# Scores and their gradients in groups of four chunks, bf16 scores out of PSUM, and the rescale of P on GpSimd, in the backward pass of a two-branch layer

## The chip, the core and the metric

The kernel runs on one core of a Trainium2 chip. The metric is device time in microseconds (us) of one execution. The engines are named as in the profile: PE is TensorE (its weight loads are PEld), DVE is VectorE, ACT is ScalarE, POOL is GpSimd, SP is the queue that issues most DMAs.

## The reference

One layer with two branches, forward and all gradients, for x of shape 2 × 4000 × 144 in bf16 (B = 2, T = 4000, D = 144, K = 5). The attention branch is what the change is about:

```python
xa = _layernorm(x, axis=-1)
qkv = jnp.einsum('btd,de->bte', xa, w_qkv)
q, k, v = (qkv[..., :D].copy(), qkv[..., D:2 * D].copy(), qkv[..., 2 * D:].copy())
scores = jnp.einsum('btd,bsd->bts', q, k) * D ** (-0.5)
p = _softmax(scores, axis=-1)
attn = jnp.einsum('bts,bsd->btd', p, v)
glob = jnp.einsum('btd,de->bte', attn, w_att_out)
```

The local branch (GELU, a layer norm, a 5-tap convolution over time, a product) gives `loc`; both are joined, pass another 5-tap convolution, and a last matmul adds them to x. The kernel returns that output and, from `grad_out`, the gradients of x and of the seven weights.

## The kernel before, in words

**Tiles.** The two batches are done one after the other, with the merge of the first overlapping the start of the second. In a batch T is cut into NB = 32 row-tiles of PB = 125 tokens. The scores of a tile, 125 × 4000, are made in eight chunks of CH = 500 columns, worked on as four pairs c2 = 0 to 3. A pair lies in one PSUM buffer `ps` of two banks, one bank a chunk; there are two such buffers (`ps_sg`), three smaller ones for all else (`ps_w`: X, projections, transposes, local steps) and one for Y and Z (`ps_yz`).

**The contraction over D = 144** has 16 rows more than the array's 128. The first 128 are `xaT_m` (columns of all tokens) against `qt` slot 0 or 2; the other 16 lie at partitions 96 to 111 of the array `R`, whose other rows hold zeros or are met by zeros: the narrow rows of a tile are put at columns 96 to 111 of a zeroed buffer `qrr`, transposed into slots 1 and 3 of `qt`, and multiplied as a second full 128-row matmul (L741, L791).

**The loop** (`phase_att`) goes over t = 0 to 32, in eight steps each. The first four make the scores of tile t (`S_pair`): four matmuls, then DVE writes −S into `Pbuf` with a running row minimum (L745 for the first pair, L747 for the others), and ACT makes the exponential from PSUM into `Pbuf` with the minimum so far as bias (L748), so the score buffer is held until ACT is done. The last four make dP = dY·V' of tile t − 1 (`dP_pair`): four matmuls, then one DVE pass (dP − delta) · P into `Sbuf` (L794). Steps 2 and 3 also hold the two halves of Y(t − 1) = P·[x, 1] (L768), after which DVE makes 1/rowsum and delta (L774, L778), ACT makes `yn` and the scaled queries `QBs` (L780, L782). At step 3, `rescale(t)` brings the first three pairs of P to the last minimum: factors f by ACT (L753), two pairs on DVE (L757), one on ACT (L759), and then one DMA transpose of the tile's P into `PT` (L760), which Y reads. Steps 6 and 7 hold the halves of Z(t − 2) from `ST` (L810), the DMA transpose of `Sbuf`.

**Between them** stand the X groups (L849): for three blocks of tokens, products of P and S of two tiles with `QBs`, twelve matmuls or more, added by DVE to the accumulator `acc` in SBUF (L855); the projection of the next tile's queries (`jit_mm`, L707 to L711, and its transposes `jit_tr`, L722); and the local branch, whose steps (`local_units`, 16 groups of two tiles a batch) are spread over the tiles by a running count.

**The order.** The code's order is the priority order; a scheduler takes from it, for each engine, the next instruction that is ready by its estimates. The engines' queues run in order. `high_priority` and `issue_after`, which the change uses, move instructions in that order.

## Time and profile before

| what | us |
|---|---|
| three runs | 1459.54, 1456.56, 1458.52 (median 1458.52) |
| the profiled execution, its own time | 1457.65 |
| its span from first to last instruction | 1455.9 |
| granted clock of TensorE, mean | 0.99 of full speed |

The page of the profile gives for each engine the busy time and its share of the span, and the span in 40 slices, each digit the busy tenths of a slice. A group row reads: line, engine, operation, output<-inputs, shapes, count | busy us, mean ns of one | idle time of the engine just before them and what ended it. A row of a source line gives ns as minimum/median/maximum, then the first and last start in us. A timeline row gives start us, duration us, engine, line and operation; behind it in brackets idle time and its releaser. A matmul's duration includes its way through the array, so what a matmul costs in a stream is read from start to start. A waits row reads: who waited for whom, us in total, times, longest.

### The profile page before, as it was taken

The page shows a single profiled execution, that of the slowest core. Times are in us where ns is not written, and L with a number is a line of the kernel's source. Part 1 is how long each engine was busy: PE and PEld are TensorE (multiplying, and loading weights), DVE is VectorE, ACT ScalarE, POOL GpSimd, SP SyncE. Part 2 cuts the span into 40 slices and gives each one's busy share as a digit, 9 for nine tenths or more (in the row PEclk, how much of TensorE's full clock was granted, in tenths as well). Part 3 has the DMA queues.
Part 4 walks back from the last instruction along what each step waited for, and adds up shares of the span by engine and source line. Part 5 has one row for each costly group of instructions (what it writes and reads, how often), then busy time and mean ns, then how long its engine had stood idle before and what let it go on. Part 6 is the DMA issues. An engine that isn't in the chain of part 4 may idle for free. (4 is left out here: it accounts for less than half of the span.)

```text
span 1455.9 us, 38963 instructions
## 1 busy us (share of the span) xinstructions
PE 1371.7 (94%) x16186; PEld 1180.2 (81%) x16186; DVE 1179.7 (81%) x2747; ACT 863.0 (59%) x1636; POOL 289.0 (20%) x515
## 2 busy tenths in 40 slices
PE   5999999999999999988887999999999999999898
PEld 3778888888888888887865888888888888888797
DVE  7799988888898988869457988888888888887754
ACT  6766666666666665525456666666666666554281
POOL 8411011111111110148212012111111111111420
PEclk9999999999999999999999999999999999999999
DMA  3586767666666666774236676666676666776712
GB/s 109 104 139 118 119 119 122 123 123 112 110 119 114 117 109 123 125 170 131 81 67 121 123 123 116 110 122 126 113 122 117 122 110 119 132 123 115 209 37 64
DMA packets 559391, 170.37 MB, mean 117 GB/s; under 512 B 542447, under 2 KB 554113, under 8 KB 559172
## 3 DMA queue, kind: packets, MB, share of 16 engines
q1 hardware_dynamic: 553578, 155.57, 58.0%
q0 software_dynamic: 5088, 12.11, 3.3%
q8 instruction: 126, 2.06, 0.6%
q14 instruction: 51, 0.42, 0.1%
q10 hardware_dynamic: 548, 0.21, 0.1%
HBM read 21.04 MB, written 14.12 MB: 24 GB/s over the span
## 5 line engine op out<-in xcount | busy, mean ns | idle before, releaser
L794 DVE SCALAR_TENSOR_TENSOR Sbuf<-ps,delta,Pbuf 125x1000 bf16<-125x1000 f32 x256 | 320.2, 1256 | 31.1 <-PE ps L791 29.0
L849 PE MATMUL X<-QBs,Sbuf 125*125 125x144 bf16 x2048 | 303.0, 226 | 6.5 <-DVE acc L855 2.7
L849 PE MATMUL X<-QBs,Pbuf 125*125 125x144 bf16 x2048 | 301.9, 226 | 0.0
L849 PEld LDWEIGHTS <-Pbuf 125*125 125x125 bf16 x2048 | 262.0, 137 | 15.2 <-issue 10.8
L849 PEld LDWEIGHTS <-Sbuf 125*125 125x125 bf16 x2048 | 261.9, 137 | 5.1
L855 DVE TENSOR_TENSOR acc<-X,acc 125x432 f32<-125x432 f32 x372 | 204.3, 552 | 36.5 <-PE X L849 35.7
L740 PE MATMUL ps<-xaT_m,qt 128*125 128x500 bf16 x512 | 193.2, 377 | 9.9 <-ACT Pbuf L748 6.7
L790 PE MATMUL ps<-xaT_m,qt 128*125 128x500 bf16 x512 | 191.8, 375 | 9.1 <-ACT Pbuf L748 6.1
L741 PE MATMUL ps<-R,qt 128*125 128x500 bf16 x512 | 192.3, 376 | 0.6 <-DVE R L357 0.4
L791 PE MATMUL ps<-R,qt 128*125 128x500 bf16 x512 | 191.0, 373 | 0.0
L768 PEld LDWEIGHTS <-PT 125*125 125x125 bf16 x2048 | 149.2, 138 | 28.2 <-DMA PT<-Pbuf 10.1
L768 PE MATMUL yz<-xa_aug,PT 125*125 125x145 bf16 x2048 | 152.4, 228 | 8.6 <-DMA PT<-Pbuf 8.5
L810 PEld LDWEIGHTS <-ST 125*125 125x125 bf16 x1984 | 143.8, 138 | 16.8
L810 PE MATMUL yz<-xa_aug,ST 125*125 125x144 bf16 x1984 | 147.7, 228 | 0.0
L745 DVE TENSOR_SCALAR_CACHE_REDUCE Pbuf<-ps 125x1000 bf16<-125x1000 f32 x64 | 76.7, 1198 | 23.7 <-PE ps L741 23.1
L595 POOL TENSOR_TENSOR A_dwc<-l_fl,A_dwc 128x512 f32<-128x512 f32 (+2 forms) x48 | 35.7, 743 | 295.9 <-ACT l_fl L594 295.9
L741 PEld LDWEIGHTS <-qt 128*125 128x125 bf16 x512 | 70.4, 137 | 28.7 <-issue 9.2
L791 PEld LDWEIGHTS <-qt 128*125 128x125 bf16 x512 | 69.6, 136 | 29.6 <-issue 9.3
L740 PEld LDWEIGHTS <-qt 128*125 128x125 bf16 x512 | 70.2, 137 | 22.2 <-issue 1.8
L790 PEld LDWEIGHTS <-qt 128*125 128x125 bf16 x512 | 69.7, 136 | 22.7 <-DVE Sbuf L794 2.1
L465 POOL TENSOR_SCALAR l_a<-l_sq 125x576 bf16<-125x576 bf16 x32 | 21.5, 671 | 299.5 <-ACT l_sq L463 260.2
L814 ACT ACTIVATE zn<-yz,rl 125x144 bf16<-125x144 f32 x64 | 24.1, 376 | 95.0 <-PE yz L810 94.9
(801 smaller groups left out, 3089.8 us busy)
## 6 DMA issues: line engine op xcount, KB each, us to landing
Yn_d<-yn SPq DMA_DIRECT2D x64, 35.2 KB
Zn_d<-zn SPq DMA_DIRECT2D x64, 35.2 KB
ug_d<-ugr SPq DMA_DIRECT2D x32, 70.3 KB
xo<-in_x_dram SPq DMA_DIRECT2D x16, 140.6 KB
out_dram<-dxo SPq DMA_DIRECT2D x16, 140.6 KB
go_h<-in_grad_out_dram POOLq DMA_DIRECT2D x4, 504.0 KB, 6.7
Zn<-Zn_d SPq DMA_DIRECT2D x4, 504.0 KB
PT<-Pbuf SPq DMA_TRANSPOSE x64
```

The costliest lines, as they stand in the source:

```text
L595: nc.gpsimd.tensor_tensor(acc, fl[0:rows, 0:n], acc, op=ALU.add)
L740: nc.tensor.matmul(ps[:, h, 0:CH], qt[:, 0, :], xaTm[:, cs], start=True, stop=False)
L741: nc.tensor.matmul(ps[:, h, 0:CH], qt[:, 1, :], R[:, cs], start=False, stop=True)
L745: nc.vector.tensor_scalar(pdst, src, -1.0, None, op0=ALU.mult, op1=ALU.min, accum_out=nm[:, 0:1])
L768: nc.tensor.matmul(Y, PT[0:PB, j, 0:PB], xaa[:, j, 0:D + 1], start=(j == 0), stop=(j == NB - 1))
L790: nc.tensor.matmul(ps[:, h, 0:CH], qt[:, 2, :], xaTm[:, cs], start=True, stop=False)
L791: nc.tensor.matmul(ps[:, h, 0:CH], qt[:, 3, :], R[:, cs], start=False, stop=True)
L794: nc.vector.scalar_tensor_tensor(sdst, ps[:, :, 0:CH].rearrange("p h (a b) -> p h a b", b=PB), DL[i][:], psrc, op0=ALU.subtract, op1=ALU.mult)
L810: nc.tensor.matmul(Z, ST[0:PB, j, 0:PB], xaa[:, j, 0:D], start=(j == 0), stop=(j == NB - 1))
L814: nc.scalar.activation(zn[:, 0:D], Z, ACT.Copy, scale=RL.pop(i)[:])
L849: nc.tensor.matmul(X[:, jj, :], l, r, start=(n_ == 0), stop=(n_ == len(ops) - 1))
L855: nc.vector.tensor_tensor(av, X[:, 0:nj, :], av, op=ALU.add)
```

## The change

- **Groups of four** (`quad`): a pair of S of tile t and a pair of dP of tile t − 1 are made together. First the four 128-row matmuls (L744), then the four remainder matmuls (L750), each of only 16 rows. The narrow rows of the tokens are copied by eight more SP transfers a batch into a new array `XR`, chunk c at partitions 32·(c mod 4); the tile's narrow rows are put at the four matching places by two POOL copies (`rems`), so that the four matmuls lie in four different groups of 32 partitions and in four banks. The pairs of dP run in the order 1, 0, 3, 2.
- **Scores leave PSUM after DVE** (`S_exp`): DVE writes −S as bf16 with the pair's own minimum (L770, a constant in place of the earlier minimum), a small DVE operation takes the running minimum (L772), and ACT makes the exponential in place in SBUF (L773).
- **dP** (`PdP`): for three pairs ACT copies dP from PSUM into `Sbuf` as bf16 (L780) and DVE multiplies by P in SBUF, 1024 wide with the padding (L782); for the fourth DVE multiplies straight from PSUM (L778). delta is no longer subtracted there; it enters as −delta/rowsum (`nd`, L815) into Z (`ty` on ACT, then L846 on DVE in place of ACT) and into `QBs`, which takes four POOL operations now (L822 to L826).
- **Rescale** on POOL, three operations of 1024 (L791), except for a batch's last tile and the first two of the second batch.
- **Order**: Y of t − 1 stands at the end of a tile after the last group, Z of t − 2 after the second group, the `ST` transpose goes in two halves; the end of a batch is reordered so that its last dP doesn't wait for Y.
- **Local steps**: six of ACT's element-wise operations a group of two tiles go to POOL (two of 576, four of 144 elements).

The core of the diff:

```diff
+            for c in (2 * g, 2 * g + 1):
+                nc.sync.dma_start(S.XR[32 * (c % 4):32 * (c % 4) + DR, (c // 4) * CH:(c // 4 + 1) * CH], S.R[96:112, c * CH:(c + 1) * CH])
...
-        nc.scalar.activation(q_[:], th[:], ACT.Copy, scale=0.5, bias=0.5)
+        nc.gpsimd.tensor_scalar(q_[:], th[:], 0.5, 0.5, op0=ALU.mult, op1=ALU.add)
...
+        def quad(work, stacked=True):
+            pp = [ps_sg.tile([PB, 2, 512], F32, tag="sg", name="ps") for _ in range(len(work) // 2)]
+            for r, (i, h, c) in enumerate(work):
+                mm = nc.tensor.matmul(pp[r // 2][:, r % 2, 0:CH], QT[i][:, 3 * h, :], xaTm[:, c * CH:(c + 1) * CH], start=True, stop=False)
+            with tc.issue_after(mm.ins), tc.high_priority():
+                for r, (i, h, c) in enumerate(work):
+                    q = c % 4 if stacked else 3
+                    rs = slice(32 * q, 32 * q + DR)
+                    xr = XR[rs, (c // 4) * CH:(c // 4 + 1) * CH] if stacked else R[rs, c * CH:(c + 1) * CH]
+                    nc.tensor.matmul(pp[r // 2][:, r % 2, 0:CH], QT[i][rs, 1 + (q // 2 + h) % 2, :], xr, start=False, stop=True)
...
-                nc.vector.tensor_scalar(pdst, src, -1.0, nm[:, c2 - 1:c2], op0=ALU.mult, op1=ALU.min, accum_out=nm[:, c2:c2 + 1])
-            nc.scalar.activation(pdst, src, ACT.Exp, bias=nm[:, c2:c2 + 1], scale=1.0)
+            nc.vector.tensor_scalar(pdst, src, -1.0, 3.0e38, op0=ALU.mult, op1=ALU.min, accum_out=nm[:, o:o + 1])
+            if c2:
+                nc.vector.tensor_tensor(nm[:, c2:c2 + 1], nm[:, c2 - 1:c2], nm[:, o:o + 1], op=ALU.min)
+            nc.scalar.activation(pdst, pdst, ACT.Exp, bias=nm[:, c2:c2 + 1], scale=-1.0)
...
-            nc.vector.scalar_tensor_tensor(sdst, ps[:, :, 0:CH].rearrange("p h (a b) -> p h a b", b=PB), DL[i][:], psrc, op0=ALU.subtract, op1=ALU.mult)
+            if direct:
+                nc.vector.tensor_tensor(pv(Sbuf, i % NDB, c2), src, pv(Pbuf, i % NPB, c2), op=ALU.mult)
+            else:
+                nc.scalar.copy(pv(Sbuf, i % NDB, c2), src)
+                sc = Sbuf[0:PB, i % NDB, c2 * 1024:(c2 + 1) * 1024]
+                nc.vector.tensor_tensor(sc, sc, pchunk(i % NPB, c2), op=ALU.mult)
...
+                if not quick:
+                    nc.gpsimd.tensor_scalar(p_, p_, f[:, c2:c2 + 1], 1.0, op0=ALU.mult, op1=ALU.mult)
...
+            products(0)
+            if ok(t - 3):
+                zt_tr(t - 3)
+            loc(0.25)
+            if ok(t + 1):
+                jit_mm(t + 1)
+            loc(0.5)
+            x(1)
+            products(1)
+            for h in range(2):
+                if ok(t - 2):
+                    Z_half(t - 2, h)
+            st_half(0)
+            x(1)
+            loc(0.6)
+            if t < NB:
+                products(2)
+            if ok(t + 1):
+                jit_tr(t + 1)
+            x(1)
+            loc(0.95)
+            x(1)
+            if t < NB:
+                products(3)
+                for h in range(2):
                     if ok(t - 1):
+                        Y_half(t - 1, h)
+            loc(1.0)
             x(6)
+            st_half(1)
+            if t < NB:
+                rescale(t, t == NB - 1)
```

**How it moves instructions.** TensorE before, at the start of a tile: the end of an X group, one pair of S (`xaT_m` the 128 rows, `R` the remainder, `ps_7145` the score buffer), with the transposes of zn (L822) behind it.

```order
L849 MATMUL X_7116<-QBs_120,Pbuf_116 125x144
L740 LDWEIGHTS qt_6998
L740 MATMUL ps_7145<-xaT_m_64,qt_6998 125x500
L741 LDWEIGHTS qt_6998
L741 MATMUL ps_7145<-R_65,qt_6998 125x500
L740 LDWEIGHTS qt_6998
L740 MATMUL ps_7145<-xaT_m_64,qt_6998 125x500
L741 LDWEIGHTS qt_6998
L741 MATMUL ps_7145<-R_65,qt_6998 125x500
L822 LDWEIGHTS zn1_128
```

Each chunk's remainder follows its 128-row matmul directly. TensorE after, at the same place, from the third matmul of the group on: `ps_7520` and `qt_7362` are the scores of tile t, `ps_7521` and `qt_7041` the dP of tile t − 1, `XR` the copied narrow rows.

```order
L744 LDWEIGHTS qt_7041
L744 MATMUL ps_7521<-xaT_m_64,qt_7041 125x500
L744 LDWEIGHTS qt_7041
L744 MATMUL ps_7521<-xaT_m_64,qt_7041 125x500
L750 LDWEIGHTS qt_7362
L750 MATMUL ps_7520<-XR_66,qt_7362 125x500
L750 LDWEIGHTS qt_7362
L750 MATMUL ps_7520<-XR_66,qt_7362 125x500
L750 LDWEIGHTS qt_7041
L750 MATMUL ps_7521<-XR_66,qt_7041 125x500
L750 LDWEIGHTS qt_7041
L750 MATMUL ps_7521<-XR_66,qt_7041 125x500
```

The four remainder matmuls now stand in one row, with nothing between them, and two score buffers are taken in one go. DVE before, from the end of Y (rl, dj) through the dP passes of a tile to the next tile's first scores:

```order
L774 RECIPROCAL rl<-yz 125x1
L778 SCALAR_TENSOR_TENSOR dj,delta<-yz,rl,qb_122 125x144
L794 SCALAR_TENSOR_TENSOR Sbuf<-ps,delta,Pbuf 125x8x125
L757 TENSOR_SCALAR Pbuf<-Pbuf,f 125x8x125 x2
L855 TENSOR_TENSOR acc<-X,acc 125x3x144
L794 SCALAR_TENSOR_TENSOR Sbuf<-ps,delta,Pbuf 125x8x125 x2
L855 TENSOR_TENSOR acc<-X,acc 125x3x144
L855 TENSOR_TENSOR acc<-X,acc 125x144
L794 SCALAR_TENSOR_TENSOR Sbuf<-ps,delta,Pbuf 125x8x125
L855 TENSOR_TENSOR acc<-X,acc 125x3x144
L745 TENSOR_SCALAR Pbuf,nm__8734<-ps 125x8x125
```

DVE after, from a tile's last group (its scores L770, its direct dP product L778) through the end of Y to the next tile's first groups:

```order
L770 TENSOR_SCALAR Pbuf,nm__7530<-ps 125x8x125
L778 TENSOR_TENSOR Sbuf<-ps,Pbuf 125x8x125
L772 TENSOR_TENSOR nm__7530<-nm__7530 125x1
L810 RECIPROCAL rl<-yz 125x1
L813 SCALAR_TENSOR_TENSOR dj,delta<-yz,rl,qb_122 125x144
L815 SCALAR_TENSOR_TENSOR nd<-delta,rl 125x1
L887 TENSOR_TENSOR acc<-X,acc 125x144
L770 TENSOR_SCALAR Pbuf,nm__7858<-ps 125x8x125
L887 TENSOR_TENSOR acc<-X,acc 125x3x144
L782 TENSOR_TENSOR Sbuf<-Sbuf,Pbuf 125x1024
L887 TENSOR_TENSOR acc<-X,acc 125x3x144
L470 TENSOR_TENSOR l_z<-l_a,l_hs 125x576
```

The rescale has left DVE's queue, and scores and dP products now alternate. POOL after, around a rescale: local steps (`l_` names, `gd`), the four operations on `QBs`, and the three on P.

```order
L467 TENSOR_SCALAR l_a<-l_sq 125x576
L472 TENSOR_SCALAR l_a<-l_sq 125x576
L475 TENSOR_SCALAR l_q<-l_th 125x576
L518 TENSOR_SCALAR l_th<-l_q 125x576
L487 COPY ur_1003<-l_hg 125x288
L486 TENSOR_TENSOR rsr_1015<-ve,mhalf 125x2
L504 TENSOR_SCALAR gd_987<-l_hg,rsr_1015 125x144 x2
L822 TENSOR_SCALAR QBs<-qb_123,rl 125x144
L824 TENSOR_SCALAR g_8158<-qb_123,rl 125x144
L825 TENSOR_SCALAR g_8157<-qb_123,nd 125x144
L826 TENSOR_TENSOR QBs<-g_8157,g_8158 125x144
L791 TENSOR_SCALAR Pbuf<-Pbuf,f 125x1024 x3
```

Before, POOL had of these rows only L465 and L470 (here L467 and L472), the copy and the small operation behind them (here L487 and L486); the rescale now stands behind the operations on `QBs`, and these behind the local steps.

194 lines of the change are left out of this document (96 added, 98 removed).

## The prediction

> **What bounds the kernel now.** First the busy totals and the 40 slices of the page.
>
> ```profile
> PE 1371.7 (94%) x16186; PEld 1180.2 (81%) x16186; DVE 1179.7 (81%) x2747; ACT 863.0 (59%) x1636; POOL 289.0 (20%) x515
> PE   5999999999999999988887999999999999999898
> ```
>
> TensorE is busy in nearly every slice except the head, the change of batch and the tail. Then a window of twenty row-tiles, and the exponentials of two tiles nine apart, which give the period.
>
> ```profile
> core 0: us, PE busy (x) PEld busy (x) DVE busy (x) ACT busy (x) POOL busy (x), PEclk, DMA share, GB/s
> 200.00:584.00 384.00, 376.32 (x4395) 322.75 (x4393) 330.93 (x714) 243.32 (x460) 48.38 (x75) 1.00 0.66 117
> L748 ACT ACTIVATE Pbuf<-ps,nm__3071 x4: 1096/1097/1097, 189.4 to 197.1; 125x1000 bf16<-125x1000 f32 x4
> L748 ACT ACTIVATE Pbuf<-ps,nm__5885 x4: 1096/1097/1106, 362.0 to 369.9; 125x1000 bf16<-125x1000 f32 x4
> ```
>
> A tile takes (362.0 − 189.4)/9 = 19.18 us. Divided by 384/19.18 = 20.0 tiles, the window gives per tile DVE 16.55, ACT 12.2, POOL 2.4, and TensorE idle (384 − 376.32)/20 = 0.38. So TensorE's own stream sets the period: shorter matmuls there are worth their whole time, and DVE has 2.6 us to spare. The waits table names what little idle time the scores' buffers cause.
>
> ```profile
> PE ps L740 <- ACT Pbuf L748: 6.7, 11, 1.5
> PE ps L790 <- ACT Pbuf L748: 6.1, 16, 0.9
> ```
>
> That is 12.8 us in the whole run: letting scores leave PSUM earlier can't bring more than that by itself.
>
> **The change part by part.** *The remainder matmuls.* The stream of TensorE now:
>
> ```profile
> 401.33 0.38 PE L740 MATMUL ps<-xaT_m,qt 128*125 128x500 bf16 x1
> 401.54 0.37 PE L741 MATMUL ps<-R,qt 128*125 128x500 bf16 x1
> 401.75 0.38 PE L740 MATMUL ps<-xaT_m,qt 128*125 128x500 bf16 x1
> 401.97 0.37 PE L741 MATMUL ps<-R,qt 128*125 128x500 bf16 x1
> 402.18 0.28 PE L707 MATMUL pj<-RW,R 128*125 128x288 bf16 x1
> ...
> 403.36 0.23 PE L849 MATMUL X<-QBs,Pbuf 125*125 125x144 bf16 x1
> 403.42 0.38 PE L740 MATMUL ps<-xaT_m,qt 128*125 128x500 bf16 x1
> ```
>
> Start to start a 500-column matmul takes 0.211 ((402.18 − 401.33)/4), a short one 0.06. Four remainder matmuls (two S, two dP) cost 4 × 0.211 = 0.844 now. Afterwards each uses 16 rows in another group of 32 partitions and another bank. No row of this trace has two matmuls side by side; what a matmul on few rows costs among full ones, one place shows:
>
> ```profile
> 1444.34 0.48 PE L1145 MATMUL po<-VUl,YT 128*125 128x144 bf16 x5
> 1444.65 0.23 PE L1147 MATMUL po<-VUsl,YS 80*125 80x144 bf16 x1
> 1444.71 0.48 PE L1145 MATMUL po<-VUl,YT 128*125 128x144 bf16 x5
> 1445.12 0.17 PE L1356 MATMUL fpt<-ident,dwmb 16*5 16x16 bf16 x1
> 1445.22 0.28 PE L1147 MATMUL po<-VUsl,YS 80*125 80x144 bf16 x1
> 1445.33 0.48 PE L1145 MATMUL po<-VUl,YT 128*125 128x144 bf16 x5
> ```
>
> The six L1145/L1147 take 0.37 to the next block (1444.34 to 1444.71); with the 16-row matmul between them 0.62. Of the extra 0.25, 0.06 is its own slot, so 0.19 goes into the change to few rows and back. The group of four then costs 0.19 + 0.211 = 0.40 if all run together, 0.19 + 0.211 + 3 × 0.06 = 0.58 if each starts a short slot after the one before, 0.19 + 0.844 = 1.03 if they don't overlap. I take 0.49, midway between the first two: saving 4 × (0.844 − 0.49) = 1.42 per tile. The Trainium skill (TensorE: Matmul & The Clock Gate, "Part 3: Packing small matmuls — row/col tiling") gives 3.07 times the speed for four matmuls of 32 rows and 512 columns; by it the group would be 0.844/3.07 + 0.19 = 0.465, an estimate, and the time 6 us lower; no run here shows it yet.
>
> *The groups.* A pair of S and a pair of dP now start together and fill both score buffers, and the next group starts with S. Between the first group and the second stand only about 21 short matmuls (two transposes, twelve of a local step, seven of the projection): 21 × 0.06 = 1.3 us.
>
> ```profile
> L794 DVE SCALAR_TENSOR_TENSOR Sbuf<-ps,delta,Pbuf 125x1000 bf16<-125x1000 f32 x256 | 320.2, 1256 | 31.1 <-PE ps L791 29.0
> L745 DVE TENSOR_SCALAR_CACHE_REDUCE Pbuf<-ps 125x1000 bf16<-125x1000 f32 x64 | 76.7, 1198 | 23.7 <-PE ps L741 23.1
> L757 DVE TENSOR_SCALAR Pbuf<-Pbuf,f 125x1000 bf16<-125x1000 bf16 x128 | 57.1, 489 | 10.0 <-ACT f L753 9.9
> L855 DVE TENSOR_TENSOR acc<-X,acc 125x432 f32<-125x432 f32 x310 | 185.8, 602 | 21.7 <-PE X L849 20.9
> L468 DVE TENSOR_TENSOR l_z<-l_a,l_hs 125x576 bf16<-125x576 bf16 x32 | 14.6, 455 | 6.8 <-POOL l_a L465 6.8
> L578 DVE SCALAR_TENSOR_TENSOR l_dd<-pd,rsr,l_w 125x144 bf16<-125x144 f32 x64 | 21.6, 359 | 0.2 <-ACT l_w L572 0.2
> L759 ACT ACTIVATE Pbuf<-Pbuf,f 125x1000 bf16<-125x1000 bf16 x64 | 73.0, 1140 | 0.1
> L392 ACT COPY xaT_m<-pt 128x1000 bf16<-128x1000 bf16 x8 | 7.9, 992 | 16.9 <-PE pt L391 16.9
> ```
>
> The score buffer comes free after the last matmul's tail (0.38 − 0.21 = 0.17) and DVE's pass (1.20): 1.37, just over the gap, so 0.1 of wait at least. If DVE is inside an accumulator add (0.60) when the scores come, 0.7. I take 0.4 per tile, midway; between the later groups stand at least forty short matmuls (Z's 32 and an X group, or three X groups), 2.4 us or more, so I give them no wait. Behind a waiting L744 the local and projection matmuls that would fill the gap are queued.
>
> *DVE*, per tile: two rescales go (−2 × 0.489), four dP passes go (−4 × 1.256); one direct product comes at 1.20, the price of the 1000-element pass L745, and three from SBUF at 0.455 × 1024/576 = 0.81 each; the zn step 0.36. The three minima and nd are small operations, priced by this reciprocal (the second row is for the moves, below):
>
> ```profile
> 761.57 0.17 DVE L774 RECIPROCAL rl<-yz 125x1 f32<-125x1 f32 x1 [2.33 <-PE yz L768]
> 796.10 0.63 PE L768 MATMUL yz<-xa_aug,PT 125*125 125x145 bf16 x3 [4.82 <-DMA PT<-Pbuf]
> ```
>
> So 4 × 0.17 = 0.68, and DVE ends at 16.55 − 6.00 + 3.63 + 0.36 + 0.68 = 15.2 of 18 us: costs nothing while it keeps to that. *ACT* gets three copies out of PSUM (3 × 0.99) and loses a rescale (1.14): 12.2 + 2.97 − 1.14 = 14.0 even before the local steps that leave it. It hides behind TensorE.
>
> *POOL*: the 144- and 16-element rows give 0.836 ns an element, so 1.11 for 1024; by the 576-element row 0.671 × 1024/576 = 1.19.
>
> ```profile
> L219 POOL TENSOR_SCALAR sWm<-raw,cols x10: 369/375/388, 13.5 to 22.7; 128x144 bf16<-128x144 bf16 x10
> L261 POOL TENSOR_SCALAR sr<-two,cols x20: 264/268/512, 33.1 to 38.3; 128x16 bf16<-128x16 bf16 x20
> L465 POOL TENSOR_SCALAR l_a<-l_sq 125x576 bf16<-125x576 bf16 x32 | 21.5, 671 | 299.5 <-ACT l_sq L463 260.2 <-issue 15.3 <-DVE Sbuf L794 12.6
> ```
>
> Three rescales 3.3 to 3.6, four QBs steps 1.5, and per tile half of two 576-element and four 144-element local steps, 1.4: POOL goes from 2.4 to about 9, with room. Two things queue behind it: the PT transpose on SP, needed only at the next tile's end, and the first group's dP product, which reads P's second chunk and so needs POOL's second rescale. By my estimate that ends 7 us after a tile's last group (Y's 32 × 0.06, three DVE steps and their hand-overs 1.2, QBs 1.5, two rescales 2.2), when the copy of that dP pair is about ready too. A short miss lies within the 0.4.
>
> *Moves.* Y moves to the tile's end, so the waits for PT at the start of the second batch (2.33 and 4.82, above) should go: −7; bounds 0 and the 8.5 of all such waits. The two ST halves, the row copies on SP and the new order in the tail I cost at nothing (±5): SP issues few transfers.
>
> *Sum.* 1.42 − 0.40 = 1.02 per tile × 62 tiles (1 to 31 of the first batch, 2 to 31 of the second, and the lone pairs at the ends as one) = 63; with the 7 for PT, 70. From the profiled execution's 1457.65, which is 0.87 below the runs' median and not told from it, comes 1388.
>
> **The rivals.** *Full gain* (0.40 a group, no new waits): 62 × 4 × 0.444 = 110, +7: 1341. For it: waits are absorbed by other matmuls that the scheduler moves up; against: the 1.3 us gap.
>
> *Most is handed back* by the first group's successors: if each of the four groups waits 0.3 for DVE, 1.2 of the 1.42 is gone, 14 + 7 remain: 1437. For it: both buffers are taken at once.
>
> *Port lock, slower.* DVE's operations with two inputs in SBUF stall while POOL streams:
>
> ```profile
> L474 DVE TENSOR_TENSOR l_hg<-l_q,l_hs x32: 439/457/877, 68.8 to 1246.8; 125x576 bf16<-125x576 bf16 x32
> 789.12 0.66 POOL L470 TENSOR_SCALAR l_a<-l_sq 125x576 bf16<-125x576 bf16 x1
> 789.22 0.88 DVE L474 TENSOR_TENSOR l_hg<-l_q,l_hs 125x576 bf16<-125x576 bf16 x1
> ```
>
> L474 took 0.88 beside the POOL operation, 0.457 otherwise: 0.42 lost. After the change about 13 such DVE operations a tile (three dP products, five local ones, five small) face a POOL that is busy half the time. If every one lost 0.42, that is 5.5: DVE 20.7, 1.5 over the old period, and +93: 1551. It decides from 19.18 − 15.2 = 4.0 us a tile; by the share of time that POOL is busy I expect 2 to 3. The Trainium skill (SBUF — State Buffer, "Who interferes with whom") states the same rule: a DVE instruction with two SBUF inputs is locked out by a GpSimd instruction that reads SBUF, and speaks so against this change; L474's row agrees.
>
> *The row groups don't run side by side* (the change doesn't do what its layout is for): 1.03 a group, +0.19 × 4 × 62 = 47, −7: 1498. Against: four row groups, four banks, nothing shared.
>
> **How the numbers follow.** Forecast 0.50, its own range from 0.40 a group with the 0.4 (86 + 7: 1365) to 0.58 with it (41 + 7: 1410); full gain 0.18; handed back 0.16; port lock 0.08; no overlap 0.08. The range leaves out the last two (0.16) and the end of handed back: 1340 to 1440. What a measurement can tell here is 0.2%, 3 us: the runs lie 1456.56 to 1459.54. Faster: 0.50 + 0.18 + 0.14 = 0.82; same 0.03 (handed back to the last us); slower 0.15.
>
> **What would show it.** Right: L750 starts follow each other by 0.06 or less, and the first one follows L744 by less than 0.4; the period is 18.1 to 18.2; TensorE's waits for DVE at L744 come to some 0.4 a tile; POOL's L791 take 1.1, DVE's L782 0.8. Wrong: L750 0.21 apart (no overlap); L782 and the local products at 1.2 and DVE without gaps (port lock); L744 waiting at every group (handed back); no waits at L744 and a period of 17.4 (full gain).

## The result, and the profile after

The changed kernel takes 1520.96 us (median of 4 runs, 1516.75 to 1523.70), the kernel before 1458.64 (4 runs): a ratio of 1.0427 (95% interval 1.0400 to 1.0454). The forecast was 1388, range 1340 to 1440. The profiled execution took 1523.70, its span is 1521.9.

First the busy totals of the page after, and its slices of TensorE and of the granted clock.

```profile
PE 1338.4 (88%) x16190; PEld 1090.4 (72%) x16190; DVE 1130.9 (74%) x2947; ACT 848.0 (56%) x1451; POOL 756.1 (50%) x1267
PE   6888899898998998989888899999899989998598
PEclk9889999999999999999888999999999999999799
```

No engine is fuller than before, except POOL; TensorE fell from 94% to 88% of a longer span, and its clock is no longer 9 in every slice. The next two rows are the same window, most of the first batch, before and then after.

```profile
111.80:600.00 488.20, 478.76 (x5590) 410.85 (x5591) 421.96 (x912) 309.69 (x583) 59.89 (x94) 1.00 0.66 118
```

```profile
111.80:600.00 488.20, 442.44 (x5362) 356.52 (x5362) 389.14 (x959) 289.56 (x486) 252.37 (x400) 0.98 0.65 114
```

From the first exponential of tile 4 to that of tile 31 a tile takes 19.22 us before and 19.81 after. With it the window's rows split into two numbers that the rest of this text goes by: TensorE's **stream** (busy share times period) went from 18.85 to 17.95 us a tile, its **idle time** from 0.37 to 1.86. The matmul time was saved, and more than that was lost to waits.

By stretches, each from the start of a tile's first exponential to another's (us):

| stretch | before | after | difference |
|---|---|---|---|
| tiles 1 to 4 of the first batch (head) | 54.3 | 69.9 | +15.6 |
| 4 to 31 | 519.0 | 534.8 | +15.8 |
| 31 to the second batch's first | 129.7 | 137.5 | +7.8 |
| first four tiles of the second batch | 70.5 | 68.4 | −2.1 |
| its tiles 4 to 31 | 512.7 | 528.6 | +15.9 |
| from there to the end of the span | 128.0 | 141.0 | +13.0 |

So half of the 66 us is in the steady tiles, where 63 were to be gained, and half at the ends, where the prediction had 7 to gain and else nothing (±5).

**The group of four did what it should.** One group of the timeline (start, duration, engine, line), and the two forms of L750 in the rows of that line:

```profile
333.01 1.01 PE L744 MATMUL ps<-xaT_m,qt 128*125 128x500 bf16 x4
333.95 0.43 PE L750 MATMUL ps<-XR,qt 16*125 16x500 bf16 x4
334.31 0.23 PE L731 MATMUL pt<-ident,qb 125*128 125x125 bf16 x1
...
L750 PE MATMUL ps<-XR,qt x1016: 419/420/673, 37.2 to 1400.0; 16*125 16x500 bf16 x170
L750 PE MATMUL ps<-R,qt x8: 617/646/672, 19.5 to 34.4; 16*125 16x500 bf16 x8
```

The group takes 1.30 (334.31 − 333.01). The four 128-row matmuls need 4 × 0.211 = 0.844 of it, so the remainders cost 0.46; 0.49 was predicted. The four L750 start within 0.01 us (four of 0.42 lie in the 0.43 of the row), so they do run side by side. (The second row also shows a slip in the text above: the two tiles that go their own way are the first batch's first, not the second's. The count of 62 is the same.)

**Where TensorE waits.** The waits table of the whole run, its first rows, and behind the dots the first two of the window 111.8 to 600:

```profile
PE ps L744 <- DVE Pbuf L770: 42.7, 68, 2.2
PE yz L804 <- DMA PT<-Pbuf: 24.2, 6, 17.8
PE X L881 <- DVE acc L887: 14.4, 17, 2.0
PE pd L494 <- DVE acc L887: 9.7, 10, 2.3
...
PE ps L744 <- DVE Pbuf L770: 16.3, 30, 1.6
PE X L881 <- DVE acc L887: 8.2, 8, 2.0
```

Before, the scores' buffers cost 12.8 in all. Now TensorE comes for them 68 times before DVE has been through, and it also waits for PSUM that holds X until DVE has added it (L887). The rows of the window added up by what TensorE waits for, per tile: the score buffers 0.70 (0.13 before), a smaller buffer that one of DVE's adds L887 still reads 0.65 (0.07 before), ACT 0.27 (0.15), the local step L580 on DVE 0.13 (none). So less than half of the idle time stands at the score buffers. Of that part 0.36 lies ahead of a tile's second group, 0.23 ahead of the fourth and 0.09 ahead of the two others (idle time at the matmuls L744, tiles 4 to 31). What DVE does meanwhile, at the start of a tile, and POOL beside it:

```profile
345.33 1.20 DVE L770 TENSOR_SCALAR_CACHE_REDUCE Pbuf<-ps 125x1000 bf16<-125x1000 f32 x1 [0.60 <-PE ps L750]
...
347.80 2.67 DVE L782 TENSOR_TENSOR Sbuf<-Sbuf,Pbuf 125x1024 bf16<-125x1024 bf16 x1 [1.26 <-POOL Pbuf L791]
...
345.10 1.12 POOL L791 TENSOR_SCALAR Pbuf<-Pbuf,f 125x1024 bf16<-125x1024 bf16 x1
346.18 0.49 POOL L597 TENSOR_TENSOR A_dwc<-l_fl,A_dwc 80x144 f32<-80x144 f32 x1
346.65 2.21 POOL L791 TENSOR_SCALAR Pbuf<-Pbuf,f 125x1024 bf16<-125x1024 bf16 x2
348.82 1.10 POOL L597 TENSOR_TENSOR A_dWiT<-l_fl,A_dWiT 96x432 f32<-96x432 f32 x1
```

The product of the first group waits 1.26 for POOL's second rescale (a local sum of POOL's stands between the first and the second), and then takes 2.67 in place of 0.7, until POOL is through with the third rescale and another local sum. The next scores wait in DVE's queue behind it.

**The clock.** A long wait can be paid for a second time. Here TensorE waited 1.62, and the group after it ran at half speed (rows of the timeline, then the window around it, whose third number from the right is the granted clock):

```profile
544.93 0.58 PE L530 MATMUL pt<-ident,gd 125*128 125x125 bf16 x4 [1.62 <-DVE l_dd L580]
545.30 0.62 PE L535 MATMUL pt<-ident,gd_rem 125*80 125x125 bf16 x4
546.04 1.82 PE L744 MATMUL ps<-xaT_m,qt 128*125 128x500 bf16 x4
547.79 0.57 PE L750 MATMUL ps<-XR,qt 16*125 16x500 bf16 x4
...
545.00:550.00 5.00, 4.88 (x43) 3.37 (x43) 4.12 (x8) 3.66 (x7) 2.07 (x4) 0.69 0.49 94
```

Four matmuls start over 1.75 us instead of 0.94. In the window from 111.8 to 600 the clock is 1.00 before and 0.98 after; 0.02 of 19.81 is about 0.4 us a tile. The first batch's steady tiles have five such drops (from 189.7, 220.5, 486.7, 544.7 and 578.9 us), each of 3.4 us, with a wait of 1.6 to 2.4 us ahead of it. The length of the wait alone doesn't decide: waits of 1.65 and 1.79 us (to 299.7 and 396.4) have no drop behind them. In the trace's record of the clock all drops of a run begin on one grid of 3.41 us, and what the nine drops in the steady tiles of both batches have in common is the grid window ahead of them: TensorE was idle for 1.66 to 2.22 us of it, about half or more; in no other window of full clock there was it idle for more than 1.79. In the example it is the stretch from 541.3 to 544.7, 1.76 busy of 3.40, with 0.50 granted in the next. The Trainium skill (TensorE: Matmul & The Clock Gate, "Part 1: The HAM clock gate (the "warmup" mystery)") says that the array falls to half clock after an idle window of about 3.4 us; in this trace windows of that length that were idle for about half went ahead of the drops.

**The ends.** In the head POOL's operations for the weights stand behind the copies of the third tile's narrow rows, and in the end TensorE waits 17.8 us for the last tile's P transpose (POOL and PE rows, then SP's queue and PE):

```profile
57.10 0.83 POOL L725 COPY qr<-qb 125x64 bf16<-125x64 bf16 x2 [21.19 <-ACT qb L715]
57.92 5.57 POOL L261 TENSOR_SCALAR sr<-two,cols 128x16 bf16<-128x16 bf16 x20
61.05 0.26 PE L265 MATMUL hps<-raw,sr 128*80 128x144 bf16 x1 [1.00 <-POOL sr L261]
...
1398.26 11.15 SPq L796 DMA_TRANSPOSE PT<-Pbuf  x1
1425.18 0.38 PE L804 MATMUL yz<-xa_aug,PT 125*125 125x145 bf16 x1 [17.81 <-DMA PT<-Pbuf]
```

Before, L261 ran from 33.1 to 38.3; POOL now idles 21.19 first. The clock is lower at these places too: 0.85 in the mean of the head stretch (1.00 before), 0.91 at the change of batch (0.96), 0.85 in the second batch's first four tiles (0.95), 0.94 from there to the end (0.96). What share of the lost time this is, no run separates.

### The profile page after: what moved, and what is told of

It is laid out like the page before. It is cut to its first block, busy times and chain, and to the rows that moved or that the text cites. A ratio compares the mean times of both kernels' runs of the same rounds, so it can differ in the third digit from the quotient of the medians.

```text
span 1521.9 us, 40065 instructions
## 1 busy us (share of the span) xinstructions
PE 1338.4 (88%) x16190; PEld 1090.4 (72%) x16190; DVE 1130.9 (74%) x2947; ACT 848.0 (56%) x1451; POOL 756.1 (50%) x1267
## 5 line engine op out<-in xcount | busy, mean ns | idle before, releaser
L770 DVE TENSOR_SCALAR_CACHE_REDUCE Pbuf<-ps 125x1000 bf16<-125x1000 f32 x256 | 305.8, 1195 | 54.8 <-PE ps L750 54.6
L744 PE MATMUL ps<-xaT_m,qt 128*125 128x500 bf16 x1024 | 283.5, 389 | 49.0 <-DVE Pbuf L770 42.7
L881 PEld LDWEIGHTS <-Sbuf 125*125 125x125 bf16 x2048 | 266.2, 139 | 15.9 <-issue 15.0
L887 DVE TENSOR_TENSOR acc<-X,acc 125x432 f32<-125x432 f32 x372 | 202.9, 550 | 58.6 <-PE X L881 57.5
L782 DVE TENSOR_TENSOR Sbuf<-Sbuf,Pbuf 125x1024 bf16<-125x1024 bf16 x189 | 175.0, 926 | 75.9 <-POOL Pbuf L791 60.6
L780 ACT CAST Sbuf<-ps 125x1000 bf16<-125x1000 f32 x189 | 188.5, 998 | 68.6 <-PE ps L750 67.2
L791 POOL TENSOR_SCALAR Pbuf<-Pbuf,f 125x1024 bf16<-125x1024 bf16 x180 | 206.5, 1159 | 8.3 <-ACT f L787 7.7
L744 PEld LDWEIGHTS <-qt 128*125 128x125 bf16 x1024 | 129.9, 141 | 95.5 <-issue 61.8
L822 POOL TENSOR_SCALAR QBs<-qb,rl 125x144 bf16<-125x144 bf16 x64 | 25.3, 396 | 190.3 <-DVE rl L810 189.9
L750 PE MATMUL ps<-XR,qt 16*125 16x500 bf16 x1016 | 115.1, 431 | 0.0
L750 PEld LDWEIGHTS <-qt 16*125 16x125 bf16 x1024 | 37.5, 130 | 105.3 <-issue 105.3
L778 DVE TENSOR_TENSOR Sbuf<-ps,Pbuf 125x1000 bf16<-125x1000 f32 x67 | 80.2, 1197 | 0.5 <-PE ps L750 0.3
L574 POOL TENSOR_SCALAR l_w<-gd,nc,c 125x144 f32<-125x144 bf16 x64 | 31.4, 498 | 75.3 <-DVE nc L570 70.4
L1208 PE MATMUL po<-VUl,YT 128*125 128x144 bf16 x640 | 54.1, 231 | 7.0 <-ACT goT L350 7.0
```

Of the source, the lines that this page charges most:

```text
L744: mm = nc.tensor.matmul(pp[r // 2][:, r % 2, 0:CH], QT[i][:, 3 * h, :], xaTm[:, c * CH:(c + 1) * CH], start=True, stop=False)
L750: nc.tensor.matmul(pp[r // 2][:, r % 2, 0:CH], QT[i][rs, 1 + (q // 2 + h) % 2, :], xr, start=False, stop=True)
L770: nc.vector.tensor_scalar(pdst, src, -1.0, 3.0e38, op0=ALU.mult, op1=ALU.min, accum_out=nm[:, o:o + 1])
L778: nc.vector.tensor_tensor(pv(Sbuf, i % NDB, c2), src, pv(Pbuf, i % NPB, c2), op=ALU.mult)
L780: nc.scalar.copy(pv(Sbuf, i % NDB, c2), src)
L782: nc.vector.tensor_tensor(sc, sc, pchunk(i % NPB, c2), op=ALU.mult)
```

## The experiments

All are the changed kernel with the edits named. Stream and idle time are us a tile, worked out as above from the window 111.8 to 600 and the period of tiles 4 to 31 of the first batch, in the profiled execution; its time lies within 7 us of the median, but for e2's (1525.21). The ratio is taken over all runs, against runs of the kernel before from the same time, so it is not that of two medians of the table.

| run | median us | ratio to before (95% interval) | period | stream | idle |
|---|---|---|---|---|---|
| before | 1458.64 | | 19.22 | 18.85 | 0.37 |
| changed | 1520.96 | 1.0427 (1.0400 to 1.0454) | 19.81 | 17.95 | 1.86 |
| e1 rescale on DVE and ACT | 1504.11 | 1.0317 (1.0294 to 1.0339) | 19.69 | 17.74 | 1.95 |
| e2 dP order | 1511.07 | 1.0378 (1.0325 to 1.0431) | 19.75 | 17.97 | 1.78 |
| e3 dP order, direct first | 1514.55 | 1.0381 (1.0357 to 1.0404) | 19.77 | 17.88 | 1.89 |
| e4 local steps on ACT | 1491.32 | 1.0221 (1.0199 to 1.0242) | 19.36 | 17.65 | 1.71 |
| e5 Z between groups 1 and 2 | 1537.74 | 1.0555 (1.0534 to 1.0576) | 19.99 | 18.00 | 1.99 |
| e6 head and end | 1517.26 | 1.0402 (1.0377 to 1.0427) | 19.82 | 17.96 | 1.86 |
| e7 one row group | 1561.47 | 1.0710 (1.0676 to 1.0745) | 20.35 | 19.85 | 0.50 |
| c1 e1, e4, e5, e6 together | 1514.02 | 1.0391 (1.0371 to 1.0411) | 19.65 | 17.93 | 1.72 |
| e8 pairs | 1596.67 | 1.0951 (1.0933 to 1.0970) | 21.18 | 19.72 | 1.46 |
| e9 no dP product | 1471.54 | 1.0091 (1.0061 to 1.0120) | 19.07 | 17.82 | 1.25 |
| e10 e1 and e4 | 1489.18 | 1.0219 (1.0186 to 1.0252) | 19.45 | 17.70 | 1.75 |
| e11 pairs, e1 and e4 | 1514.65 | 1.0385 (1.0358 to 1.0411) | 19.77 | 19.30 | 0.47 |
| e12 Z split | 1507.89 | 1.0352 (1.0328 to 1.0376) | 19.58 | 17.74 | 1.84 |
| e13 e10, Z split, head | 1491.44 | 1.0238 (1.0210 to 1.0265) | 19.61 | 17.83 | 1.78 |
| e14 e13, direct in group 2 | 1478.83 | 1.0136 (1.0113 to 1.0159) | 19.45 | 17.80 | 1.65 |
| e15 e14, zn transposes late | 1475.50 | 1.0142 (1.0106 to 1.0177) | 19.15 | 17.82 | 1.33 |
| e16 e15, projection late | 1459.34 | 1.0029 (1.0011 to 1.0046) | 18.88 | 17.77 | 1.11 |
| e17 e16, no direct product, head | 1457.76 | 1.0014 (0.9994 to 1.0034) | 18.99 | 17.80 | 1.19 |

**e1: the rescale back on DVE and ACT.**

```diff
-                rescale(t, t == NB - 1)
+                rescale(t, True)
```

> The changed kernel with the rescale of P back on DVE (two operations) and ACT (one) in every tile; all else as changed. Theory 1 (the rescale on POOL at a tile's end: the first dP product stands in DVE's queue behind it, L782 waited 60.6 us for L791 in all, and is then locked out while POOL goes on; scores and accumulator adds queue behind it, TensorE waits and its clock drops): about 1 us of TensorE's 1.65 us of waits per tile goes and most clock drops with it, 1430 to 1460 us, and L782 at 0.7 to 0.75 us instead of 0.93. Theory 2 (the group of four itself: both score buffers are taken at once, and too little stands between the first and the second group): no gain, 1515 to 1530, since DVE gets 1 us more per tile. Theory 3 (the local steps on POOL hold up DVE): 1500 or more.

It gained 17 us, but not as theory 1 has it. The lock and the wait are gone: the row of L782, which in the changed kernel has 926 ns and 60.6 us of waits for L791, reads

```profile
L782 DVE TENSOR_TENSOR Sbuf<-Sbuf,Pbuf 125x1024 bf16<-125x1024 bf16 x189 | 132.3, 700 | 20.4 <-ACT Sbuf L780 19.0
```

and yet TensorE's idle time in e1 is 1.95 a tile, the period 19.69. Most of the gain lies outside: 7.3 in the second batch's first four tiles (61.1) and 7.8 at the end (133.2). POOL's rescale was the plainest wait in the profile and not what set the period. (DVE has the rescale to do again here; e3, below, is the test without that.)

**e2 and e3: the dP order.** Pairs 3, 0, 1, 2; in e3 the direct product is also the first group's. The first half of the S transpose moves behind the third group.

```diff
-                ps = quad(S_work(t, q) + (dP_work(t - 1, q ^ 1) if ok(t - 1) else []))
+                ps = quad(S_work(t, q) + (dP_work(t - 1, (q + 3) % 4) if ok(t - 1) else []))
...
-                    PdP(t - 1, q ^ 1, ps[1], q == 3)
+                    PdP(t - 1, (q + 3) % 4, ps[1], q == 0)
```

> The changed kernel with the dP pairs in the order 3, 0, 1, 2 instead of 1, 0, 3, 2, so that the first group's product reads the pair that is not rescaled; the first half of the S transpose moves behind the third group. The rescale stays on POOL and the product still has two inputs in SBUF. Theory 1, if the wait for the rescale's result is what counts: 1450 to 1490, the wait of L782 for L791 falls from 60 us to under 20. If instead the lock counts (L782 runs while POOL rescales): 1500 to 1520, L782 stays above 0.9 us. Theory 2: 1515 to 1525.

> As the run before it (dP order 3, 0, 1, 2), and the direct product from PSUM is the first group's instead of the last group's: it neither waits for the rescale nor has two inputs in SBUF. Theory 1 in either form: 1430 to 1465. Theory 2: 1515 to 1525, since the first group's two buffers are released by two DVE passes one after the other.

10 and 6 us, periods 19.75 and 19.77. e2's time lies in the range given for the lock, but L782 takes 836 ns in the mean, not above 0.9. In e3 L782 takes 705 ns and waits 3.2 us in the whole run, so wait and lock are both gone without any more work for DVE, and the idle time is 1.89: theory 1 falls in both its forms.

**e4: the local steps back on ACT.** Four lines, six operations for a group of two tiles, as in the kernel before.

> The changed kernel with the six local steps of a group of two tiles back on ACT; the rescale stays on POOL. Theory 3 (these steps hold up DVE): 1450 to 1480. Theory 1: they lie elsewhere in the tile than the rescale, 1500 to 1520. Theory 2: 1515 to 1530, ACT has 1.8 us more per tile.

The largest single gain, 30 us, though short of theory 3's 1450 to 1480. The window reads

```profile
111.80:600.00 488.20, 445.05 (x5490) 359.72 (x5489) 398.77 (x986) 338.58 (x586) 207.52 (x327) 1.00 0.66 116
```

with a clock of 1.00: the idle time is only a little less (1.71), but no drop of the clock falls into the window, and the stream is 0.3 shorter. The waits for L580 ahead of two of the five drops, such as the 1.62 shown above, are gone; L580 is a DVE operation that needs POOL's L574. The longest waits are no shorter than before: five of 2.2 to 2.6 us. The longest, from 460.5 to 463.1, lies across two windows of the clock's grid, which are idle for 1.72 and 1.41 us. In the second batch's steady tiles the mean clock is 0.98 in e4 as in the changed kernel, so the 0.3 of the first batch may in part be luck.

**e5: Z between the first two groups.**

```diff
+            for h in range(2):
+                if ok(t - 2):
+                    Z_half(t - 2, h)
             x(1)
             products(1)
-            for h in range(2):
-                if ok(t - 2):
-                    Z_half(t - 2, h)
```

> The changed kernel with Z of tile t - 2 (32 matmuls, 2 us) between the first and the second group instead of behind the second. Theory 2 (too little between these two groups, so that TensorE comes back for the score buffers before DVE has emptied them): the wait of L744 for L770, 42.7 us in the changed kernel, falls below 20 us and the period from 19.7 to 19.2 or less, 1485 to 1500 us. Theory 3 (POOL and ACT are loaded so that DVE comes late all over the tile): 1510 to 1525, the waits move to other places.

17 us slower. Z now comes too soon for its transposed S, and the scores' wait grew (the changed kernel has 42.7 in the first of these rows, and none to speak of in the second):

```profile
PE ps L744 <- DVE Pbuf L770: 64.9, 56, 6.2
...
PE yz L842 <- DMA ST<-Sbuf: 28.5, 31, 2.9
```

**e6: the two ends.**

```diff
-                M.open_early(ST)
+                M.open_early(PT)
...
-                rems(nc.gpsimd.tensor_copy, i, h)
+                rems(nc.scalar.copy if i == 2 and head is not None else nc.gpsimd.tensor_copy, i, h)
```

> Two edits at two ends of the program, to be read apart by the time of each stretch: the merge's loads are released by the last P transpose instead of the last S transpose (end of both batches), and the copies of the third tile's narrow rows are made on ACT instead of POOL (head). If the 17.8 us wait for P at the end comes from these loads, which start just ahead of the transpose, the stretch behind the last scores falls from 141 us to 125 to 130. If the head's 15.6 us come from POOL's work for the weights, which stands 21 us behind these copies in POOL's queue, the stretch of tiles 1 to 4 falls from 69.9 to 56 to 60. Together 1490 to 1500 us; if neither is the cause, 1515 to 1525.

The wait for P at the end goes, as expected, and another takes its place, since the loads that come later are needed soon:

```profile
PE yz L804 <- DMA PT<-Pbuf: 3.4, 5, 1.3
...
PE Hps L1129 <- POOL go_r L1096: 8.4, 2, 4.4
```

The last stretch falls from 141.0 to 136.1, the change of batch rises from 137.5 to 144.6. In runs that don't touch this place the last stretch is 133 to 135 as well (e1, e3, e4) or 145 (e2), and the longest wait for P there is anything from 3.9 (e3) to 18.4 us (e2). So what sets this wait is not shown. The head gained 4.1 of 15.6: L261 runs from 35.6 again, but POOL's next operations for the weights then stand behind the first tile's operations on QBs.

**e7: one row group.** All four remainders use rows 96 to 111.

```diff
-        def quad(work, stacked=True):
+        def quad(work, stacked=False):
```

> The changed kernel with the four remainder matmuls in one and the same group of 32 rows, one after the other. If the four row groups run side by side, L750 starts 0.21 apart here, a group takes 0.58 us longer and a tile 2.3 us of TensorE time more; with TensorE idle 2 us a tile part of that is covered: 1560 to 1640 us. If the row groups bring nothing, no difference: 1515 to 1530.

1561, a ratio of 1.071, at the lower end. L750 starts 0.23 apart and a group takes 1.93 in place of 1.30. The stream grows by 1.90 a tile and the idle time falls to 0.50:

```profile
111.80:600.00 488.20, 476.12 (x5227) 368.95 (x5226) 384.70 (x940) 283.87 (x477) 248.43 (x398) 1.00 0.63 111
```

So the row groups are worth what they were said to be worth, and a longer stream hides the same waits, with both score buffers still taken at once: at the score buffers 0.18 a tile is left of 0.70, elsewhere about 0.3 of 1.06.

**c1: everything back together, with Z whole between the groups.**

> All of these together: the rescale on DVE and ACT, the local steps on ACT, Z between the first two groups, the merge's loads behind the last P transpose, the head's copies on ACT; what stays of the change are the groups of four with their row groups, the exponential from SBUF, the dP copies on ACT and the folded delta. If the causes add up (17 + 30 + 25 + 25 us off 1521): 1420 to 1440, faster than the kernel before. If DVE and ACT are then the limit (DVE 16, ACT 14.5 of 18 us a tile): 1450 to 1470.

1514, 25 more than e1 and e4 give together (e10, below): the single gains don't add up, and e5's part is a loss.

**e8 and e11: pairs instead of groups of four**, a pair of scores and, one filler later, a pair of dP; e11 with e1 and e4 as well.

```diff
-                ps = quad(S_work(t, q) + (dP_work(t - 1, q ^ 1) if ok(t - 1) else []))
-                S_exp(t, q, ps[0])
-                if ok(t - 1):
-                    PdP(t - 1, q ^ 1, ps[1], q == 3)
+                S_exp(t, q, quad(S_work(t, q))[0])
+
+            def products_d(q):
+                if t < NB and ok(t - 1):
+                    PdP(t - 1, q ^ 1, quad(dP_work(t - 1, q ^ 1))[0], q == 3)
```

> The changed kernel with its groups of four cut in two: a pair of scores (two 128-row matmuls, two remainders in two row groups) and, one filler later, a pair of dP, so that the two score buffers are taken and given back in turn again; all the work on POOL, ACT and DVE as in the changed kernel. TensorE's own stream is then about as long as in the kernel before (each pair pays the change to few rows, some 19.0 us a tile). Theory 4 (what costs the waits is that a group takes both score buffers, so TensorE can't run ahead of DVE by a pair): TensorE idles less than 0.6 us a tile, period 19.2 to 19.5, 1475 to 1500 us, faster than the changed kernel although TensorE has 1.6 us a tile more to do. If DVE, POOL and ACT are late whatever the buffers do (theory 3, in general form): idle stays near 1.9, period 20.3 or more, 1550 to 1580.

> Pairs instead of groups of four, and the rescale and the local steps back on DVE and ACT: of the change there remain the exponential from SBUF, the dP copies, the folded delta, and the moves of Y and Z. By theory 4 with POOL's part taken out too: 1455 to 1480 us, about the kernel before, with what is left lying in the head and the ends. If the exponential from SBUF or the dP copies cost something of their own: 1490 or more.

e8 is the slowest of all (1597): with POOL's work as changed, the waits stay (idle 1.46) and the stream is 19.72, so theory 4 alone does not explain the changed kernel. Against e7, whose stream is nearly as long (19.85) and whose groups still take both buffers, pairs even idle more, 1.46 against 0.50, though their order differs as well. e11 has POOL's work taken away too:

```profile
111.80:600.00 488.20, 476.50 (x5406) 354.57 (x5405) 386.37 (x1014) 360.39 (x595) 122.03 (x241) 1.00 0.65 115
```

Idle 0.47, near the 0.37 of the kernel before; against e10, which has the groups of four and so another place for each pair of dP, 1.28 less idle and 1.60 more stream. Grouping by four saves 1.6 us of matmul time a tile and gives 1.3 of it back as waits. That the waits come from taking both buffers at once is not shown by this: from e7 to the changed kernel 1.90 less stream, with the grouping the same, brought 1.36 more idle time; at that rate, 1.60 less would bring 1.14 of the 1.28 by itself. The pairs' stream is also 0.45 longer than before; a pair takes 0.873 from its first matmul to the next instruction, 0.845 before, which makes 0.22 of it in eight pairs.

**e9: without the product on DVE** (three of four pairs of S hold dP itself).

```diff
                 nc.scalar.copy(pv(Sbuf, i % NDB, c2), src)
                 sc = Sbuf[0:PB, i % NDB, c2 * 1024:(c2 + 1) * 1024]
-                nc.vector.tensor_tensor(sc, sc, pchunk(i % NPB, c2), op=ALU.mult)
```

> The changed kernel without the multiplication of the copied dP by P (three of four pairs; S then holds dP itself, so part of the computation is left out). DVE has some 2.8 us a tile less to do and never stands behind POOL's rescale. Theory 5 (TensorE waits because DVE's queue, 16 of 19.7 us busy and locked out by POOL, reaches the scores' passes and the adds late): period 17.5 to 18.3, 1410 to 1450 us. Theory 4 alone, with the passes' own latency deciding: 1490 or more.

1471.54: 50 us less, period 19.07, idle 1.25. Between the two theories: the products, with their waits for POOL, make up 0.6 of the idle time, and with DVE at 345.31 of 488.20 us, 71%, TensorE still waits three times as much as before.

**e10: e1 and e4 together.**

> The changed kernel with the rescale back on DVE and ACT and the six local steps back on ACT. If the two gains seen alone add up (17 and 30 us): 1470 to 1480. If they are one and the same (less work on POOL beside DVE): 1488 to 1495. If ACT and DVE then hold things up: 1500 or more.

1489.18, two below e4 alone, within the spread of the runs: the two gains are mostly one and the same. By stretches the part in common is at the second batch's first four tiles (61.1, 62.2 and 61.9 in e1, e4 and e10, against 68.4) and at the end (133.2, 133.3, 129.8, against 141.0). That it is less work on POOL beside DVE fits, and no run shows it apart.

**e12 to e17: mending the order.** Z split (its first half between groups 1 and 2), then on top of e10 and the head's copies (e13) the direct product in the second group (e14), the transposes of zn behind the third group (e15), the projection behind the second (e16), and no direct product at all (e17).

```diff
+            if ok(t - 2):
+                Z_half(t - 2, 0)
             x(1)
             products(1)
-            for h in range(2):
-                if ok(t - 2):
-                    Z_half(t - 2, h)
+            if ok(t - 2):
+                Z_half(t - 2, 1)
...
-                    PdP(t - 1, q ^ 1, ps[1], q == 3)
+                    PdP(t - 1, q ^ 1, ps[1], q == 1)
```

> The changed kernel with the first half of Z (16 matmuls, 1 us) between the first and the second group and the second half behind the second, where Z stood whole. The first half needs only the first half of the S transpose, which lies a tile back, so it has nothing to wait for. Theory 6 (what is lost is the room between the first and the second group, 1.3 us, against DVE's 1.2 to 1.4 us on the scores): the wait of L744 for L770 at the second group falls from 0.58 to under 0.2 us a tile and doesn't come back elsewhere, 1490 to 1505 us. If the wait only moves to the next group, as when Z went there whole: 1515 to 1540.

> The rescale and the local steps back on DVE and ACT, Z split as in the run before, and the head's copies on ACT. Theory 6: idle time of TensorE 1.74 to 1.0 us a tile, period 18.7, 1440 to 1460 us with the head. If the wait only moves: 1485 or more.

> As the run before, with the direct product from PSUM in the second group instead of the last: the last group's dP then leaves by ACT, and DVE has 0.5 us less between a tile's last scores and the next tile's first. If DVE's queue at the tile's end is what makes the second group late: 5 to 20 us less than the run before; if not, the same within 5 us.

e12 gained 13, just short of theory 6's 1490 to 1505, and its idle time is hardly less (1.84): 0.36 a tile ahead of the second group became 0.01, and 0.02 ahead of the third became 0.23. e13 is where e10 was (the head gained 4.4). In both the wait only moved: L744 hardly waits for L770 in e13 (2.1 us in the window), but ACT's copy of the transposed zn, which holds a buffer of the small pool, is late. e14 is 12.6 below e13. Its rows, in the window 111.8 to 600:

```profile
PE X L881 <- ACT zt L856: 7.5, 7, 1.6
PE pj L709 <- DVE acc L887: 4.2, 7, 0.8
PE ps L744 <- DVE Sbuf L778: 4.1, 6, 0.9
PE pd L562 <- ACT zt L856: 4.0, 3, 1.8
PE pj L709 <- ACT zt L856: 3.3, 6, 0.8
```

> As the run with the direct product in the second group, and the two transposes of zn with their copy on ACT (L854, L856) behind the third group instead of behind the first. There the copy stands in ACT's queue behind an exponential and a dP copy, and TensorE waited for it 17 us in a window of 25 tiles. If such single queue positions are what is left: the waits for zt go and 15 to 30 us with them, 1450 to 1465 us, about the kernel before. If every such wait taken away lets the next one show (theory 7: groups of four leave TensorE no room to run ahead of DVE and ACT, whichever comes late): 1470 to 1485.

> As the run before, and the projection of the next tile's queries (L709 to L713) behind the second group instead of ahead of it. Single positions: its waits (L709 for L887 and zt, 8 us in the same window) go too, another 5 to 15 us. Theory 7: within 8 us of the run before, either way.

e15 falls into theory 7's range (1475.50); its 3 us are within the spread of the runs, the first batch's steady tiles having gained 8.1 and the second's lost 4.8. e16 lies beyond theory 7: 16 us for moving one projection, the period at 18.88, well below the kernel before's 19.22. The largest rows that are left in the same window of e16:

```profile
PE ps L744 <- DVE Pbuf L770: 5.7, 11, 1.0
PE ps L744 <- DVE Sbuf L778: 4.5, 7, 1.2
PE pw L616 <- ACT gS L538: 2.0, 2, 1.1
```

> As the run before, with two edits that are read apart by stretch. All four dP pairs leave PSUM by ACT (no direct product on DVE): TensorE waited 10 us for L770 and L778 at the third group in a window of 26 tiles; if DVE's two passes after the second group make the third late, the period falls from 18.9 to 18.6 us; if ACT, 77% busy, then holds the score buffers instead, it rises above 19. And in the head the first tile's QBs are made on ACT and DVE, so that POOL's work for the weights no longer stands behind them: the stretch of tiles 1 to 4 falls from 66 us to 56 to 60; if the head's loss lies elsewhere it stays. Both: 1435 to 1448 us, faster than the kernel before by 0.5 to 1.5%. Neither: 1455 to 1470.

1457.76 against 1457.94 for the kernel before, a ratio over the runs of 1.0014 (0.9994 to 1.0034): no difference. The period rose to 18.99 (ACT, at 394.42 of 488.20, is as full as DVE, 393.01), the head stretch is 62.9 instead of 66.3. No version beats the kernel before. In e10 and e13 to e17 the stream stays at 17.7 to 17.8 while the idle time goes from 1.75 to 1.1. The gain that remains for e16 in the steady tiles (0.34 a tile in the first batch, 0.04 in the second, 18.95 against 18.99) is eaten by the ends: +12 in the head, +6 at the change of batch, +5 behind the second batch's last first exponential, and only −6 in its first four tiles.

## Why the prediction was wrong

- **What bounds the kernel**: right for the kernel before. TensorE's stream set the period, 18.85 of 19.22.
- **The remainder matmuls**: right, 0.46 a group against 0.49. (By the rows quoted there, 0.85/4 is 0.2125 and not 0.211, and the 86 of the sum for 0.40 is 85; neither changes the result.) That is 4 × (0.844 − 0.46) = 1.54 a tile; of it 0.90 is seen in the stream. About 0.4 went to the clock, an estimate from 0.02 of 19.81; in e4, with a clock of 1.00, 1.20 of the 1.54 is there. The rest I can only argue: the last matmul ahead of a wait counts as busy for its whole way through the array, 0.17 beyond its slot.
- **"I take 0.4 per tile", and between the later groups "I give them no wait"**: the 0.4 was about right for the gap that it priced, 0.36 ahead of the second group; none for the others was not, with 0.23 ahead of the fourth and 0.09 ahead of the others. Together TensorE waits 0.70 a tile for the score buffers, 0.57 more than before.
- **DVE at 15.2 of 18 us "costs nothing while it keeps to that", and ACT "hides behind TensorE"**: the step that failed. Idle time rose by 1.49 a tile, and the greater part of it stands at buffers for which the sum has no term: 0.65 a tile, 0.07 before, until DVE's adds have read a smaller buffer, 0.27 (0.15) until ACT is done, 0.13 for a local step on DVE. The load was right (389.14 / 488.20 × 19.81 = 15.8) and the conclusion wrong. A mean load says how much work there is, not whether it is done when it is waited for. e9, without DVE's products, regained 0.6 of the 1.49; moving single operations (e14 to e16) took the idle time from 1.78 to 1.11 with no less work for DVE or ACT.
- **The hold on both score buffers**: e11, with pairs, has score waits of 0.02 a tile where e10 has 0.86, so it may add to them. But e7 has the same hold and a longer stream, and idles 0.50. So how much of the 1.49 is due to it stays open.
- **Port lock**: the mechanism is there as the rival said (2.67 us for L782 beside POOL's operations, 926 ns in the mean against 700 in e1), and the rule of the Trainium skill cited there (SBUF — State Buffer, "Who interferes with whom") holds. Its price is far from the rival's 5.5 a tile: 189 × 0.226 = 43 us of DVE time in the run, 0.7 a tile. Its removal (e1, e3) left the idle time where it was. The time came out near that rival's side for another reason.
- **The product behind POOL's second rescale, "a short miss lies within the 0.4"**: the miss was 60.6 us of DVE time in 48 waits, up to 3.5. e2, which avoids it, gained 10, and its idle time is 0.08 less.
- **The moves, "at nothing (±5)"**: +15.6 in the head, +7.8 and +13.0 at the ends of the batches, and only −2.1 of the −7 at the second batch's start. Of the head's loss, 4.1 came back with the narrow-row copies off POOL (e6), so POOL's order there is a part of it. The rest of the head, the change of batch and the last P transpose stay open.
- **The rival "most is handed back"** had the kind of result right and its place wrong: it put 0.3 at each of the four groups, 1.2 a tile; 0.70 came there and more elsewhere. No step and no rival priced the clock.

What is shown: the row groups are worth 1.90 of stream a tile (e7); the same kernel idles less the longer its stream is (e7); POOL's local steps cost 30 us in the run (e4, with the falls of the clock and the end in it), the products on DVE 50 (e9), the place of the direct product 13 (e14) and that of the projection 16 (e16). Not settled is how much the hold on both buffers costs, and what the last 1.1 us of idle time in e16 consist of. e15 speaks for too little room for any order, e16 for a few more bad positions.

## What to carry to other kernels

When TensorE's stream is the bound, making it shorter pays only as far as the engines behind it can be late without its noticing. Price the waits at every buffer that TensorE shares with them, not only at the one that the change touches: more than half of the added waits stood elsewhere. Look at what a queue holds in front of an operation when it is waited for, at the start and the end of the program too, rather than at the engine's mean load. And don't stop at the plainest wait in the profile: without the 60.6 us of L782 the steady tiles were no faster to speak of (e3: 19.77 against 19.81), while the place of the projection, which no large row named, cost 16 us.

## What the runs showed of the hardware

- The granted clock falls to half in steps of 3.41 us on a grid that is fixed within a run. In the steady tiles of the changed kernel the nine windows ahead of such a drop were idle for 1.66 to 2.22 us; no other of full clock was for more than 1.79. So by these traces a wait can be paid twice or not, by where it falls: one of 1.62 us was followed by a drop, one of 2.60 across two windows (e4) was not.
- Four 16-row matmuls in four groups of 32 partitions and four banks start within 0.01 us and cost 0.46 us with the change to few rows and back, against 0.844 as four full ones. In one row group they start 0.23 apart, and the stream is 1.90 a tile longer. Two at a time (e11) bring nothing: 0.873 a pair against 0.845 with full matmuls.
- A DVE product of 1024 with both inputs in SBUF takes 0.70 us with POOL's rescale gone and up to 2.68 beside a busy one.
